# One set of scattering products for both small groups of the second layer's last part

## The chip, the cores and the metric

The kernel runs on one core of a Trainium2 chip. The metric is the device time of one execution in microseconds (us). TensorE (PE in the rows, PEld for its weight loads) multiplies matrices into PSUM; VectorE (DVE) and ScalarE (ACT) move and compute between PSUM and SBUF; SyncE (SP) issues the transfers between HBM and SBUF.

## The reference, cut to what matters

An attention over 4 samples of 576 tokens with 8 heads is followed by two mixture-of-experts layers of width 512 with 8 experts each. The second layer is the one that the change touches:

```python
logits = xc @ w_gate                    # xc: the tokens with x @ w_skip > 0
e_idx = np.argmax(logits, axis=1)
...
for e in range(E):
    mask = e_idx == e
    h = np.maximum(xc[mask] @ w1[e], 0.0)
    y[mask] = gate_w[mask, None] * (h @ w2[e])
out[do_compute] = xc + y
```

Each token goes to one expert; the result is weighted with the gate and added to the token.

## The kernel before

The samples are worked on one at a time, with the tokens along the free dimension: a sample's activations are X[b], four feature chunks of 128 partitions by 576 tokens. For each layer and sample the experts that got many tokens are *large groups* (class Group): all 576 tokens are multiplied with such an expert's weights, in 16 *slots* of 24 products of 288 columns, and the result is masked with the gate. Each factor is split into a high and a low part, which makes three products per block (hh, hl, wh, wl, xh, xl). The products of a slot go to one of two PSUM pairs, which ACT (hh) and then DVE (hl) evacuate.

Experts with at most 32 tokens are *small groups* (class Small). "S" is that of the first layer for sample 2 and has one expert (n = 1), "T" that of the second layer for sample 2 and has two (n = 2). Their words, in order: p (one-hot tile), g0 to g4 and gx (gather the tokens into xs), t (an expert's two layers in five steps), v (places: tiles that say where each token belongs), a (place: transposes them to pT), u (put: scatter the results). In t step 4 the expert's result is copied to two tiles, y2[0] (high part) and y2[1] (the rest). An expert's second layer leaves four blocks of 32 rows in PSUM: the two halves of the contraction for feature chunks 0 and 1, then those for chunks 2 and 3. So y2[.][:, c] holds results in rows 0 to 63 for c = 0, 1 and in rows 64 to 127 for c = 2, 3; the other half of the rows is zero from the start. put(t, i) takes chunks 2i and 2i + 1: for each and each half of the tokens it makes two products (high part, rest) of 288 columns against pT[t] into a bank of PSUM, and DVE adds that bank to X. The banks of put, of the transposes and of the router come from one pool of three (bank).

What stands where is a table written by hand, COURSE: one stage per large group, 16 lines per stage, one for each slot. Per slot: the 24 products, the split of the weights two slots later, the words ahead of the bar, the evacuation of the slot, the words behind the bar. Each engine works in that order. L4 to L7 load weights of the large group; O0 to O2 store chunks of samples; C3.x are the steps of the router for sample 3 (C3.1 logits, C3.2 transposes ptl, C3.3 one-hot oh, C3.4 counting products pp); G.1 and G.2 bring the gate into place (pgm, gT, mg); i.rw and kw prepare the router of sample 3. This document counts slots from 0, in the last stage (large group of layer 2, sample 1). The lines of that stage which speak of T are, before:

```python
    L4 G.3 | T.t03 O0.2
    | T.a0 i.rw
    L5 | T.t04 C3.1
    T.v1 | T.t10 T.u00
    L6 | T.u01 C3.2 G.1
    C3.3 | T.t11 C3.4 O0.3
    L7 C3.5 G.2 | T.t12 T.a1
    | T.t13
...
    | T.u10
    | T.u11 O1.0
```

These are slots 0 to 7, and 10 and 11 (T.t14 is in slot 9). T.v0 stands in slot 15 of the stage before. The tokens' weights of the small experts come in eight tiles each (tw, three buffers); a tile's load is issued when the product that read an earlier one is done.

Of the kernel before, what the change touches and what calls it, by code (L numbers as in the profile page):

```python
# [9 lines left out]
F32 = mybir.dt.float32  # L10
# [3 lines left out]
ALU = mybir.AluOpType  # L14
# [3 lines left out]
P = 128  # L18
NJ = 5
LAST = 64  # L20
HT = 288
TINY = 32
# [71 lines left out]
    N2 g.qn S.v0 | S.t03  # L94
    X2 | S.a0 g.qt
    N3 | S.t04
    X3 | S.u00 S.u01
    """),
    ((1, 0), """
    L4 G.3 | g.rw  # L100
# [17 lines left out]
    L4 G.3 | T.t03 O0.2  # L118
    | T.a0 i.rw
    L5 | T.t04 C3.1  # L120
    T.v1 | T.t10 T.u00
    L6 | T.u01 C3.2 G.1
    C3.3 | T.t11 C3.4 O0.3
    L7 C3.5 G.2 | T.t12 T.a1
    | T.t13
    Z B |
    | T.t14
    | T.u10
    | T.u11 O1.0
    | O2.0  # L130
    | O1.1 O2.1
    | O2.2
# [6 lines left out]
def kernel(  # L139
# [17 lines left out]
    nc = tc.nc  # L157
    B, H, S, D = q.shape
# [23 lines left out]
    def bank(name):  # L182
        return pa.tile([P, 512], F32, name=name, tag="a")

    def long_bank(name):

        return pb.tile([P, 512], F32, name=name, tag="b")
# [17 lines left out]
    def tokens(a):  # L205
        return slice(a * HT, (a + 1) * HT)
# [7 lines left out]
    iota = c32[:, C_IOTA:C_IOTA + TINY]  # L214
# [9 lines left out]
    for i, g in enumerate((w_gate, w_gate2)):  # L224
        t = cp.tile([P, NC, 32], F32, name=f"wg{i}")
        nc.gpsimd.memset(t, 0.0)
        with nc.allow_non_contiguous_dma(reason="gate weights are small"):
            nc.scalar.dma_start(out=t[:, :, 0:E], in_=g.rearrange("(c p) e -> p c e", p=P))
            if i == 1:
                nc.scalar.dma_start(  # L230
                    out=t[:, :, E:E + 1], in_=w_skip.rearrange("(c p o) -> p c o", p=P, o=1)
# [22 lines left out]
    for i in range(2):  # L254
        t = cp.tile([P, 2, P], F32, name=f"kvd{i}")
# [691 lines left out]
    with tc.tile_pool(name="fp", bufs=1) as fp:  # L947
# [3 lines left out]
        a, b = [Half(0, hh, X[0], fp, 1) for hh in range(2)]  # L951
# [158 lines left out]
    hp = ctx.enter_context(tc.tile_pool(name="hp", bufs=1, reuse_waits="tile"))  # L1110
    hp = ctx.enter_context(tc.tile_pool(name="hp", bufs=1, reuse_waits="tile"))
# [7 lines left out]
    class Small:  # L1119
# [69 lines left out]
        def expert(self, t, step):  # L1189
            if step == 0:  # L1190
                self.ph = long_bank("ph")
            elif step == 3:
                self.ph = long_bank("py")
            if step != 2:
                for i in {0: (0, 1), 1: (2, 3), 3: (4, 5), 4: (6, 7)}[step]:
                    w = self.tw.pop(8 * t + i)
                    for g in range(4):
                        if i < 4:
                            lhsT, rhs = self.xs[:, i, 32 * t:32 * t + 32], w[:, 256 * g:256 * g + 256]
                        else:  # L1200
                            lhsT = self.hT[:, g % 2, 32 * (i - 4):32 * (i - 4) + 32]
                            rhs = w.rearrange("p (u d) -> p u d", u=2)[:, g % 2, 256 * (g // 2):256 * (g // 2) + 256]
                        nc.tensor.matmul(  # L1203
                            out=self.ph[32 * g:32 * g + 32, :256], lhsT=lhsT, rhs=rhs, start=(i % 4 == 0), stop=(i % 4 == 3)
                        )
                    self.load(8 * t + i + 3)
            if step == 1:
                self.h1 = hp.tile([P, 256], F32, name="h1", tag="h1")
                nc.scalar.activation(self.h1, self.ph[:, :256], AF.Relu)
            elif step == 2:  # L1210
                pt = bank("pth")
                for u in range(2):
                    nc.tensor.transpose(pt[:, u * P:(u + 1) * P], self.h1[:, u * P:(u + 1) * P], ident)
                self.hT = hp.tile([P, 2, P], F32, name="hT", tag="h1")
                nc.vector.tensor_copy(out=self.hT, in_=pt[:, :2 * P].rearrange("p (u s) -> p u s", u=2))
            elif step == 4:
                for i in range(2):
                    sl, cs = slice(64 * i, 64 * i + 64), slice(2 * i, 2 * i + 2)
                    src = self.ph[sl, :256].rearrange("p (c d) -> p c d", c=2)
                    nc.scalar.copy(y2[0][sl, cs], src)  # L1220
                    nc.vector.tensor_sub(y2[1][sl, cs], src, y2[0][sl, cs].bitcast(F32))

        def places(self, t):
            cs = hp.tile([P, TINY], F32, name="cs2", tag="cs2")
            nc.vector.tensor_scalar(out=cs, in0=iota, scalar1=self.r["tlo"][:, t:t + 1], scalar2=None, op0=ALU.add)
            self.p4 = hp.tile([P, NJ, 4, TINY], F32, name="p4", tag="ot", bufs=3)
            bb = [P, NJ, TINY]
            for g in range(4):
                nc.vector.tensor_tensor(
                    out=self.p4[:, :, g],  # L1230
                    in0=self.r["z"].unsqueeze(2).to_broadcast(bb),
                    in1=cs.unsqueeze(1).to_broadcast(bb),
                    op=ALU.is_equal,
                )

# [8 lines left out]
            nc.tensor.transpose(pt[:, 0:LAST], p4f[:LAST, 4], ident[:LAST, :LAST])  # L1244
            nc.scalar.copy(pT[:, 4 * P:S], pt[:, 0:LAST])

        def put(self, t, i):
            for c in (2 * i, 2 * i + 1):
                for a in range(2):
                    pt = bank("pts")  # L1250
                    for n, u in enumerate(y2):
                        nc.tensor.matmul(  # L1252
                            out=pt[:, :HT], lhsT=u[:, c], rhs=self.pT[t][:, tokens(a)], start=(n == 0), stop=(n == 1)
                        )
                    x = self.x[:, c, tokens(a)]
                    nc.vector.tensor_add(x, x, pt[:, :HT])
# [83 lines left out]
    for kk, (_, plan) in enumerate(COURSE):  # L1340
        lines = plan.strip().split("\n")
        assert len(lines) == NS
        for i, line in enumerate(lines):
            before, _, after = line.partition("|")
            groups[kk].products(i)
            n = NS * kk + i + 2
# [131 lines left out]
```

## Time and profile before

| | us |
|---|---|
| runs timed | 424.27, 425.94, 426.3 (median 425.94) |
| the profiled execution | 423.36 |
| its span, first to last instruction | 421.5 |
| PE busy in the span | 396.1 (94%) |
| DVE busy | 251.8 (60%) |
| ACT busy | 182.5 (43%) |
| scattering products (L1252), 48 in all | 9.0 busy |

Sixteen of the 48 scattering products belong to S, 32 to T. Busy time of PE counts overlapping matmuls, whose ends are modelled; where PE is the bound, what a piece of work costs is read from the starts in the timeline: from its own start to that of the next kind of work on PE. Idle time stands in square brackets behind a row, with the engine whose end came last before it; that engine is inferred.

### The profile page before, as it was taken

To read this page: it belongs to the slowest core of one execution; us is meant where nothing else is said; L and a number is where in the kernel's file an instruction comes from. 1 tells how busy PE (TensorE), PEld (TensorE's weight loads), DVE (VectorE), ACT (ScalarE), POOL (GpSimd) and SP (SyncE) were. 2 spreads that over 40 slices of the span, in tenths; PEclk is the share of its full clock that TensorE was granted. 3 is DMA by queue.
4 is the path that set the end of the run, shared out by engine and by line. 5 is a ranking of instruction groups with operands and counts; after the bars stand their busy time and mean duration, and the time that the engine had idled before them with its cause. 6 is when DMAs were issued, how large, how long until landed. Compare 5 with 4: busy or idle time off the path is not lost.

```text
span 421.5 us, 8456 instructions
## 1 busy us (share of the span) xinstructions
PE 396.1 (94%) x3241; PEld 351.3 (83%) x3241; DVE 251.8 (60%) x640; ACT 182.5 (43%) x547; POOL 12.3 (3%) x46
## 2 busy tenths in 40 slices
PE   8989879999999999998999999998999999899893
PEld 4656779898999889798999888798998987799882
DVE  3875788463686755378446746367676736554431
ACT  1556666634257771423347523332375333231111
POOL 2400000000000000000000100000000000000000
PEclk9999999999999999999999999999999999999997
DMA  8819935200960300392544861117315555363134
GB/s 199 221 51 255 235 93 163 58 2 2 310 159 25 106 2 2 111 291 68 163 166 151 241 180 51 50 52 231 98 51 180 178 178 174 92 212 145 30 90 110
DMA packets 72536, 54.48 MB, mean 129 GB/s; under 512 B 18455, under 2 KB 67115, under 8 KB 72491
## 3 DMA queue, kind: packets, MB, share of 16 engines
q1 hardware_dynamic: 70536, 53.60, 44.1%
q10 hardware_dynamic: 1954, 0.31, 0.5%
q8 instruction: 26, 0.43, 0.4%
q14 instruction: 20, 0.16, 0.1%
HBM read 49.16 MB, written 4.73 MB: 128 GB/s over the span
## 4 chain that ended last, share of the span: by engine, by line
PE 70%; DVE 6%; ACT 3%; issue 2%; DVEq 0%; ACTq 0%
PE pair L860 29%; PE pair L839 21%; PE pxs L1147 2%; PE pk L437 2%; PE pl L593 2%; PE pto L1281 2%; PE ph L1203 1%; PE py L1203 1%; PE pts L1252 1%; PE px L495 1%; ACT hh L873 1%; PE ptq L463 1%; DVE wl L782 1%; PE ptx L1162 1%; DVE hl L874 1%
## 5 line engine op out<-in xcount | busy, mean ns | idle before, releaser
L860 PE MATMUL pair<-hh,wh 128*128 128x288 f32 x320 | 98.2, 307 | 0.0
L860 PE MATMUL pair<-hh,wl 128*128 128x288 f32 x320 | 94.4, 295 | 0.0
L860 PE MATMUL pair<-hl,wh 128*128 128x288 f32 x320 | 94.4, 295 | 0.0
L839 PE MATMUL pair<-xh,wh 128*128 128x288 f32 x304 | 92.9, 305 | 0.0
L839 PE MATMUL pair<-xl,wh 128*128 128x288 f32 x304 | 89.6, 295 | 0.0
L839 PE MATMUL pair<-xh,wl 128*128 128x288 f32 x304 | 89.4, 294 | 0.0
L782 DVE TENSOR_TENSOR wl<-ws,wh 128x512 fp32r<-128x512 f32 x80 | 54.9, 686 | 36.4 <-ACT wh L781 34.8
L873 ACT ACTIVATE hh<-pair 128x576 fp32r<-128x576 f32 x40 | 25.9, 647 | 88.6 <-PE pair L839 86.8
L860 PEld LDWEIGHTS pair<-hh,wh 128*128 128x128 f32 x320 | 60.4, 189 | 3.8 <-issue 2.6
L860 PEld LDWEIGHTS pair<-hl,wh 128*128 128x128 f32 x320 | 60.6, 189 | 0.1
L860 PEld LDWEIGHTS pair<-hh,wl 128*128 128x128 f32 x320 | 60.4, 189 | 0.0
L839 PEld LDWEIGHTS pair<-xh,wh 128*128 128x128 f32 x304 | 57.0, 188 | 2.3 <-issue 0.9
L874 DVE SCALAR_TENSOR_TENSOR hl<-pair,hh 128x576 fp32r<-128x576 f32 x40 | 30.2, 756 | 46.4 <-ACT hh L873 46.4
L839 PEld LDWEIGHTS pair<-xl,wh 128*128 128x128 f32 x304 | 57.1, 188 | 0.1
L839 PEld LDWEIGHTS pair<-xh,wl 128*128 128x128 f32 x304 | 57.1, 188 | 0.0
L781 ACT CAST wh<-ws 128x512 fp32r<-128x512 f32 x80 | 49.3, 620 | 2.6 <-DMA ws<-in_moe_w_dram 1.7
L334 ACT ACTIVATE eq<-qt,mx 128x64 f32<-128x64 f32 x140 | 46.7, 338 | 0.3 <-DVE mx L323 0.3
L334 ACT ACTIVATION_READ_ACCUMULATOR eq<-qt,mx 128x1 f32 x140 | 26.6, 190 | 0.0
L532 PE MATMUL pair<-warm 128*128 128x384 f16 x94 | 19.7, 359 | 1.6 <-DVE warm L949 1.6
L782 DVE TENSOR_TENSOR xl<-x,xh 128x576 fp32r<-128x576 f32 x20 | 14.9, 752 | 6.0 <-ACT xh L781 6.0
L1282 ACT COPY ot<-pto 128x256 f32<-128x256 f32 (+1 forms) x24 | 7.0, 316 | 26.0 <-PE pto L1281 26.0
L532 PEld LDWEIGHTS <-warm 128*128 128x128 f16 x94 | 9.6, 107 | 8.8 <-issue 3.2
(210 smaller groups left out, 499.9 us busy)
## 6 DMA issues: line engine op xcount, KB each, us to landing
ws<-in_moe_w_dram SPq DMA_DIRECT2D x39, 512.0 KB, 5.4
tw<-in_moe_w_dram SPq DMA_DIRECT2D x24, 512.0 KB, 4.1
kt<-in_k_dram SPq DMA_DIRECT2D x8, 512.0 KB, 7.7
qt<-in_q_dram SPq DMA_DIRECT2D x8, 512.0 KB, 6.8
out_dram<-ot SPq DMA_DIRECT2D x12, 256.0 KB, 2.7
vt<-in_v_dram SPq DMA_DIRECT2D x16, 128.0 KB, 4.5
vt<-in_v_dram SPq DMA_DIRECT2D x3, 512.0 KB
mg<-gate SPq DMA_DIRECT2D x4, 288.0 KB, 6.1
```

Source lines behind the costliest of these rows:

```text
L334: nc.scalar.activation(self.eqv[:, h, j], self.qt[:, h, j], AF.Exp, bias=self.mx[:, i:i + 1], accum_out=self.qz[:, i:i + 1])
L437: nc.tensor.matmul(out=pk[64 * g:64 * g + 64, c * D1 + o:c * D1 + o + n], lhsT=self.kt[:rows(j), 2 * c + g, j], rhs=ones32[:rows(j), 0:1] ...
L532: nc.tensor.matmul(out=pw[:, 0, :3 * P], lhsT=warm16[:, 0:P], rhs=warm16, start=True, stop=True)
L593: nc.tensor.matmul(out=pl[32 * c:32 * c + 32, :HT], lhsT=self.weights[:, c], rhs=self.chunk(c, tokens(a)), start=True, stop=True,)
L781: nc.scalar.copy(hi, src)
L782: nc.vector.tensor_tensor(out=lo, in0=src, in1=hi.bitcast(F32), op=ALU.subtract)
L839: nc.tensor.matmul(out=self.pt[:, a, :HT], lhsT=u[:, c], rhs=w[:, c, tokens(a)], start=(c == 0 and n == 0), stop=(c == NC - 1 and n == 2),)
L860: nc.tensor.matmul(out=self.pt[:, a, :HT], lhsT=p_[:, f], rhs=w[:, tokens(a)], start=(v == 0 and f == 0 and n == 0), stop=(v == 1 and f == ...
L873: nc.scalar.activation(halves(hh), src, AF.Relu)
L874: nc.vector.scalar_tensor_tensor(out=halves(hl), in0=src, scalar=0.0, in1=halves(hh).bitcast(F32), op0=ALU.max, op1=ALU.subtract,)
L1147: nc.tensor.matmul(out=self.px[:, c * self.w:(c + 1) * self.w], lhsT=self.xt[:rows(j), c * P:(c + 1) * P], rhs=self.pj[:rows(j), j], start ...
L1203: nc.tensor.matmul(out=self.ph[32 * g:32 * g + 32, :256], lhsT=lhsT, rhs=rhs, start=(i % 4 == 0), stop=(i % 4 == 3))
```

## The change

The results of T's two experts share the tiles y2. For the second expert (t = 1) the second layer writes its four blocks of rows in the order 3, 4, 1, 2, so that its results lie in the rows that the first expert's leave at zero: rows 64 to 127 for chunks 0 and 1, rows 0 to 63 for chunks 2 and 3. The places follow: v0 and v1 no longer make one tile per expert but one per pair of chunks (v0 for chunks 0 and 1 with the first expert in rows 0 to 63, v1 for chunks 2 and 3 with the second there), each from the index tiles of both experts. put(i) then multiplies y2 once with pT[i] for both experts. In the table, put of the first expert leaves slots 3 and 4, and u0 and u1 stand where u10 and u11 stood. For S nothing is different.

```diff
-    X3 | S.u00 S.u01
+    X3 | S.u0 S.u1
...
-    T.v1 | T.t10 T.u00
-    L6 | T.u01 C3.2 G.1
+    T.v1 | T.t10
+    L6 | C3.2 G.1
...
-    | T.u10
-    | T.u11 O1.0
+    | T.u0
+    | T.u1 O1.0
...
                     for g in range(4):
+
+                        o = 32 * (g ^ 2 if t and i >= 4 else g)
...
-                            out=self.ph[32 * g:32 * g + 32, :256], lhsT=lhsT, rhs=rhs, start=(i % 4 == 0), stop=(i % 4 == 3)
+                            out=self.ph[o:o + 32, :256], lhsT=lhsT, rhs=rhs, start=(i % 4 == 0), stop=(i % 4 == 3)
...
-                    sl, cs = slice(64 * i, 64 * i + 64), slice(2 * i, 2 * i + 2)
+                    o = 64 * (i ^ t)
+                    sl, cs = slice(o, o + 64), slice(2 * i, 2 * i + 2)
...
-            cs = hp.tile([P, TINY], F32, name="cs2", tag="cs2")
-            nc.vector.tensor_scalar(out=cs, in0=iota, scalar1=self.r["tlo"][:, t:t + 1], scalar2=None, op0=ALU.add)
+            cs = hp.tile([P, 2, TINY], F32, name="cs2", tag="cs2")
+            for u in range(self.n):
+                nc.vector.tensor_scalar(
+                    out=cs[:, u], in0=iota, scalar1=self.r["tlo"][:, u:u + 1], scalar2=None, op0=ALU.add
+                )
...
-                    in1=cs.unsqueeze(1).to_broadcast(bb),
+                    in1=cs[:, (g // 2) ^ t if self.n == 2 else 0].unsqueeze(1).to_broadcast(bb),
...
-        def put(self, t, i):
+        def put(self, i):
+            pT = self.pT[i if self.n == 2 else 0]
...
-                            out=pt[:, :HT], lhsT=u[:, c], rhs=self.pT[t][:, tokens(a)], start=(n == 0), stop=(n == 1)
+                            out=pt[:, :HT], lhsT=u[:, c], rhs=pT[:, tokens(a)], start=(n == 0), stop=(n == 1)
```

On PE in slot 3, before: ph is the first layer of the second expert, pts a bank of the scattering products (y0 and y1 are y2's two tiles), pair the large group's PSUM pair.

```order
L1203 MATMUL ph_4252<-tw_4090,xs_3790 32x256 x4
L1203 MATMUL ph_4252<-tw_4190,xs_3790 32x256 x4
L1252 MATMUL pts_4265<-pT_4136,y0_637 128x288
L1252 MATMUL pts_4265<-pT_4136,y1_638 128x288
L1252 MATMUL pts_4269<-pT_4136,y0_637 128x288
L1252 MATMUL pts_4269<-pT_4136,y1_638 128x288
L1252 MATMUL pts_4273<-pT_4136,y0_637 128x288
L1252 MATMUL pts_4273<-pT_4136,y1_638 128x288
L1252 MATMUL pts_4277<-pT_4136,y0_637 128x288
L1252 MATMUL pts_4277<-pT_4136,y1_638 128x288
L839 MATMUL pair1_84<-xh_124,wh0_202 128x288
```

The same place after:

```order
L1205 MATMUL ph_4254<-tw_4091,xs_3790 32x256 x4
L1205 MATMUL ph_4254<-tw_4191,xs_3790 32x256 x4
L839 MATMUL pair1_84<-xh_124,wh0_202 128x288
L839 MATMUL pair1_84<-xl_125,wh0_202 128x288
L839 MATMUL pair1_84<-xh_124,wl0_206 128x288
```

The eight scattering products between the expert's first layer and the large group's products of slot 4 are gone.

On PE at the end of slot 4, before: behind the slot's products come the second set of scattering products, the router's transposes (ptl), the gate transpose (pgm), and the products of slot 5.

```order
L1252 MATMUL pts_4312<-pT_4136,y0_637 128x288
L1252 MATMUL pts_4312<-pT_4136,y1_638 128x288
L1252 MATMUL pts_4316<-pT_4136,y0_637 128x288
L1252 MATMUL pts_4316<-pT_4136,y1_638 128x288
L1252 MATMUL pts_4320<-pT_4136,y0_637 128x288
L1252 MATMUL pts_4320<-pT_4136,y1_638 128x288
L1252 MATMUL pts_4324<-pT_4136,y0_637 128x288
L1252 MATMUL pts_4324<-pT_4136,y1_638 128x288
L605 MATMUL ptl_4328<-c32_85,lp_4202 128x128 x4
L607 MATMUL ptl4_4333<-c32_85,lp_4202 64x128
L915 MATMUL pgm_4337<-c32_85,gm_4067 5x128
L839 MATMUL pair0_83<-xh_124,wh1_203 128x288
```

The same place after:

```order
L839 MATMUL pair1_84<-xl_125,wh0_202 128x288
L839 MATMUL pair1_84<-xh_124,wl0_206 128x288
L605 MATMUL ptl_4298<-c32_85,lp_4203 128x128 x4
L607 MATMUL ptl4_4303<-c32_85,lp_4203 64x128
L915 MATMUL pgm_4307<-c32_85,gm_4068 5x128
L839 MATMUL pair0_83<-xh_124,wh1_203 128x288
L839 MATMUL pair0_83<-xl_125,wh1_203 128x288
```

The router's transposes stand directly behind the products of slot 4.

On DVE from slot 3 to the start of slot 5, before: cs and p are the place tiles, hl the evacuation, wl the split of weights, x the addition of a bank to X, L and gT the router's and the gate's results.

```order
L1225 TENSOR_SCALAR cs_4241<-c_85,tlo_183 128x32
L1229 TENSOR_TENSOR p_4243<-z_180,cs_4241 128x5x32 x4
L874 SCALAR_TENSOR_TENSOR hl<-pair_83,hh 128x576
L1256 TENSOR_TENSOR x_123<-x_123,pts 128x288 x4
L782 TENSOR_TENSOR wl_208<-ws_201,wh_204 128x512
L874 SCALAR_TENSOR_TENSOR hl<-pair_84,hh 128x576
L1256 TENSOR_TENSOR x_123<-x_123,pts 128x288 x4
L608 TENSOR_REDUCE L<-ptl 128x64
L614 TENSOR_REDUCE L<-ptl_4333 64x16
L917 COPY gT<-pgm 5x128
L782 TENSOR_TENSOR wl_209<-ws_201,wh_205 128x512
```

The same stretch after:

```order
L1229 TENSOR_SCALAR cs_4242<-c_85,tlo_183 128x32 x2
L1235 TENSOR_TENSOR p_4245<-z_180,cs_4242 128x5x32 x4
L874 SCALAR_TENSOR_TENSOR hl<-pair_83,hh 128x576
L782 TENSOR_TENSOR wl_208<-ws_201,wh_204 128x512
L874 SCALAR_TENSOR_TENSOR hl<-pair_84,hh 128x576
L608 TENSOR_REDUCE L<-ptl 128x64
L614 TENSOR_REDUCE L<-ptl_4303 64x16
L917 COPY gT<-pgm 5x128
L782 TENSOR_TENSOR wl_209<-ws_201,wh_205 128x512
```

The two blocks of four additions are gone, and the second index tile is added to the first.

## Rows read from the trace of the kernel before

**Rows 1.** The page's part 1 and the groups by line: busy, mean ns | idle before
```profile
PE 396.1 (94%) x3241; PEld 351.3 (83%) x3241; DVE 251.8 (60%) x640; ACT 182.5 (43%) x547; POOL 12.3 (3%) x46
L1252 PE MATMUL pts<-pT,y 128*128 128x288 f32 x48 | 9.0, 314 | 2.8 <-DVE x L1256 2.7
```

**Rows 2.** Timeline, end of slot 3: start us, us, engine, line, operation [idle before]
```profile
353.87 1.07 PE L1203 MATMUL ph<-tw,xs 128*32 128x256 f32 x16
...
354.65 0.76 DVE L874 SCALAR_TENSOR_TENSOR hl<-pair,hh 128x576 fp32r<-128x576 f32 x1 [0.59 <-ACT hh L873]
354.87 0.83 PEld L1252 LDWEIGHTS pts<-pT,y 128*128 128x128 f32 x6 [0.41 <-ACT hh L873]
354.87 1.62 PE L1252 MATMUL pts<-pT,y 128*128 128x288 f32 x8
...
355.95 0.30 PEld L1252 LDWEIGHTS pts<-pT,y 128*128 128x128 f32 x2 [0.25 <-DVE x L1256]
...
356.32 0.29 PE L839 MATMUL pair<-xh,wh 128*128 128x288 f32 x1
...
356.45 0.29 PE L839 MATMUL pair<-xl,wh 128*128 128x288 f32 x1
```

**Rows 3.** Timeline, end of slot 4
```profile
359.50 0.96 PE L1252 MATMUL pts<-pT,y 128*128 128x288 f32 x6
...
360.38 0.76 DVE L874 SCALAR_TENSOR_TENSOR hl<-pair,hh 128x576 fp32r<-128x576 f32 x1 [2.79 <-ACT hh L873]
361.05 1.54 DVE L1256 TENSOR_TENSOR x<-x,pts 128x288 f32<-128x288 f32 x4
...
361.55 0.53 PE L1252 MATMUL pts<-pT,y 128*128 128x288 f32 x2 [1.10 <-DVE x L1256]
...
361.92 0.66 PE L605 MATMUL ptl<-c,lp 128*128 128x128 f32 x4
...
362.64 0.08 PEld L915 LDWEIGHTS pgm<-c,gm 128*5 128x5 f32 x1 [0.23 <-DVE x L1256]
...
362.67 0.38 PE L839 MATMUL pair<-xh,wh 128*128 128x288 f32 x1
```

**Rows 4.** Timeline, end of slot 7, and the groups of tile tw (ns min/median/max)
```profile
375.93 1.07 PE L1203 MATMUL py<-tw,hT 128*32 128x256 f32 x16
...
376.92 0.19 PEld L860 LDWEIGHTS pair<-hh,wh 128*128 128x128 f32 x1 [0.41 <-ACT hh L873]
...
377.16 0.29 PE L860 MATMUL pair<-hl,wh 128*128 128x288 f32 x1
...
L1203 PE MATMUL py<-tw,hT x48: 379/379/403, 348.5 to 384.2; 128*32 128x256 f32 x48
```

**Rows 5.** Timeline, the router of sample 3 in slots 4 and 5
```profile
362.61 0.42 DVE L608 TENSOR_REDUCE L<-ptl 128x64 f32<-128x256 f32 x1
...
363.28 0.67 DVE L782 TENSOR_TENSOR wl<-ws,wh 128x512 fp32r<-128x512 f32 x1
...
364.79 0.20 DVE L632 TENSOR_TENSOR oh<-sc,fm 128x40 f16<-128x40 f32 x1
...
367.03 0.27 PE L644 MATMUL pp<-oh,c 128*128 128x32 f16 x4
```

**Rows 6.** Timeline and tile tw between 354 and 357: a weight tile for slot 5
```profile
354.56 0.33 SPq L1181 DMA_DIRECT2D tw<-in_moe_w_dram  x1
...
DMA to landing us min/median/max: 3.8/3.8/3.8
...
366.02 1.07 PE L1203 MATMUL ph<-tw,xs 128*32 128x256 f32 x16
```

**Rows 7.** Timeline of DVE, the place step of slot 3 and behind that of the stage before
```profile
352.76 0.23 DVE L1225 TENSOR_SCALAR cs<-c,tlo 128x32 f32<-128x32 f32 x1
...
336.26 0.69 DVE L782 TENSOR_TENSOR wl<-ws,wh 128x512 fp32r<-128x512 f32 x1 [0.69 <-ACT wh L781]
```

**Rows 8.** Timeline, the last two scattering products of slot 11
```profile
394.48 0.53 PE L1252 MATMUL pts<-pT,y 128*128 128x288 f32 x2 [1.22 <-DVE x L1256]
```

## The prediction

> **What bounds the kernel now.** I read the page first. TensorE (PE) is busy for 94% of the span [rows 1] and no other engine comes near. The time before is therefore set by the order of work on PE and by the few places where PE waits. The page's mean for one scattering product, 314 ns [rows 1], is not what such a product costs: matmuls are pipelined, and in the timeline a product of the same 288 columns starts 0.13 us after the one before it (356.32, then 356.45) [rows 2]. So I went to the timeline of the two slots from which products are removed, slots 3 and 4 of the last stage, and read when PE's next kind of work starts. That gives the price of the removed work with its waits.
>
> In slot 3, expert products of T end a block that starts at 353.87; the scattering products start at 354.87, the fourth pair of them waits for a PSUM bank, and the large group's products resume at 356.32 [rows 2]. In slot 4 six scattering products go out from 359.50, then PE stands still for 1.10 us: all three banks of the rotating pool are full, and the additions that empty them stand on VectorE (DVE) behind the hl evacuation (360.38, 0.76 us), so the first starts at 361.05. The last two products start at 361.55, and the router's transposes (ptl) at 361.92 [rows 3]. Both slots lie on PE, with no other engine ahead of it.
>
> **What the change removes.** 16 scattering products and 8 additions on DVE leave slots 3 and 4. Slots 10 and 11 keep 8 products each, on the same operands in size, with the same additions; their costs, a stop of 1.22 us in slot 11 included [rows 8], stay.
>
> Slot 3. What will stand behind the expert products is the large group's first product. The same succession is there in slot 7 of before: expert products at 375.93, and the second of the products behind them at 377.16, that is 1.23 us after [rows 4]. (The second is taken because the first after such a switch lasts longer.) In slot 3 that gives 353.87 + 1.23 = 355.10 where 356.45 stands now: 1.35 us gained. Of this 8 x 0.13 = 1.04 us is streaming and the rest the wait for a bank.
>
> The 0.41 us in front of the scattering products is put down to ACT [rows 2], which would make it a wait that goes with them. In slot 7 the large group's own products have the same 0.41 us behind expert products [rows 4]. I therefore keep it. The Trainium skill says the same in "TensorEngine Tiling (Array Packing)", section Tiling Modes, Key Properties: changing the tiling mode drains TensorE. By the label in slot 3 the gain would be 0.41 us larger, by that rule and the row of slot 7 it is not.
>
> Slot 4. The transposes for the router take the place of the first scattering product: 361.92 - 359.50 = 2.42 us gained. The gate transpose (pgm) after them waited 0.23 us for the last addition [rows 3]; its bank will then be one that was emptied long before, so 0.23 us more may go. I take 2.5, with 2.42 and 2.65 as ends.
>
> Sum on PE: 1.35 + 2.5 = 3.85 us, rounded 3.9. The 8 additions, in slot 4 a block of 1.54 us [rows 3], add nothing to it; what PE waited for them is in the sum. The lower bound is streaming alone, 16 x 0.13 = 2.1 us, if all the waits come back somewhere else; the upper one is 1.35 + 0.41 + 2.65 = 4.4 us.
>
> **What the change adds.** Each of T's two place steps makes two small index tiles on DVE instead of one: 0.23 us each [rows 7], 0.46 us in all. In slot 3 the next evacuation on DVE waited 0.59 us for ACT [rows 2], which hides it. The other one is at the end of the stage before, where DVE idles for 0.69 us ahead of its split at 336.26 [rows 7]. I cost both at nothing; uncovered they would cost at most 0.46 us. The second expert's second layer writes its four blocks of 32 rows in the order 3, 4, 1, 2 instead of 1, 2, 3, 4, and its results go to the other half of the rows of y. Count and size of these instructions stay. No row shows that order by itself; the order is the same cycle begun elsewhere, so I take zero, between nothing and the price of the third rival.
>
> **Who waits next.** From slot 5 on PE is 3.9 us early. Three things must be in time. The router's counting products (pp) wait for the one-hot tile oh, whose chain on DVE ran from 363.28 to 364.99, while pp came at 367.03 [rows 5]. In the new order that chain follows the slot's evacuation, which follows PE: hl would end at 360.38 + 0.76 - 1.35 = 359.8, the two reductions and the gate copy of slot 4 take 0.7 us (362.61 to 363.28), the chain 1.7 us: oh ready at about 362.2. PE wants it at 367.03 - 3.9 = 363.1. It is in time, with 0.9 us left. The weights of the second expert for slot 5 were issued at 354.56 and landed in 3.8 us, at 358.4; they are wanted at 366.02 - 3.9 = 362.1 [rows 6]. In time by 3.7 us. All later loads are issued by what PE or DVE finish from slot 5 on and move with them.
>
> At the end, slots 10 to 15 and the stores keep their order, so the whole gain reaches the last store.
>
> **The forecast.** The profiled execution took 423.36 us, its span 421.5. Less 3.9 it is 419.5. The three timed runs have a median of 425.94, above the profiled one; the mean of all four is 425.0. The gain from the median gives 422.0, from the mean 421.1. I put 421.6 between them: faster by about 0.9%.
>
> **Rivals.**
> 1. *Half the gain is given back in slot 5.* If the oh chain kept its present time (ready at 364.99) instead of moving with PE, pp would wait until then: 365.0 - 363.1 = 1.9 us returned, 2.0 us of gain left, 423.5 on the forecast's basis. For it: the margin is only 0.9 us, and the chain also has DVE's weight split before it. Against: nothing in the rows ties that chain to a fixed time; it now starts right behind the additions that go. It comes out much the same if only the streaming, 2.1 us, is gained.
> 2. *The loads become the bound.* If the tile issued at 354.56 landed later than 7.5 us after its issue, PE would stop in slot 5 for the excess, up to all 3.9 us: 421.6 to 425.5. Against: it landed in 3.8 us [rows 6], and nothing about its neighbours in the queue changes.
> 3. *Slower: the second expert's blocks no longer overlap.* 16 expert products of 0.379 us each are issued in a block of 1.07 us, since neighbours go to different blocks of 32 columns [rows 2, 4]. If the changed order lost that, they would take 16 x 0.379 = 6.1 us, 5.0 us more in each of slots 7 and 9: 10.0 - 3.9 = 6.1 us slower, 431.6. It decides once more than 1.95 us per block is lost. Against: neighbours still go to different blocks, and a block returns after four products as before.
> 4. *The saving is larger.* If the 0.41 us of slot 3 and the 0.23 us of slot 4 both went, 4.4 us: 421.1. That lies in the forecast's own range.
>
> That the change does not do what it says has no room: the order on PE shows the 16 products gone from the two slots and nothing put in their place.
>
> **How the numbers follow.** Forecast (3.4 to 4.4 us gained) 0.80, with the fourth rival in it; first rival 0.08; second 0.07; third 0.05. The range: the gain's own bounds, 3.4 to 4.4, around the two bases 425.94 and 425.0, give 420.6 to 422.5; the runs shown spread by 2 us (424.27 to 426.3), so about 1.3 us more on the low side gives 419.3; above, the first rival's 423.5 and a little of the spread give 424.2. Left out are the second rival's worse half and the third: under 2 in 10. A measurement of this kernel can tell about 0.5%, 2.1 us, from no change. The forecast and part of the first rival's spread lie beyond that: faster 0.80; the rest of the first and the second, same 0.15; the third, slower 0.05.
>
> **What would show it.** In the changed kernel's timeline the product after the expert products of slot 3 should start 1.0 us after their start, with the 0.41 us still in front of it; the router's transposes should follow slot 4's products at once, with no stop on PE until the large group's next product, about 0.6 us later; pp in slot 5 should have no wait on DVE; from slot 5 to the last store every piece should keep its distance from the one before it. In slots 7 and 9 the blocks of expert products should still last about 1.07 us. The forecast is wrong if PE stands still at ptl, pp or the expert products of slot 5, or if a later stop (slots 11 to 15) grows by what was gained.

## The result and the profile after

The changed kernel took 419.88 us (median of four runs, 419.13 to 420.29) against 425.11 for the kernel before (four runs, 423.6 to 426.3): ratio 0.9897, 95% interval 0.9873 to 0.9921, so about 1% faster. In a second comparison the ratio was 0.9883 (0.9858 to 0.9909). The profiled execution took 419.54 us; its span is 3.9 us shorter than that of before. Runs of one kernel spread with their mean granted clock (of eleven runs of the kernel before in the second comparison, seven at 0.990 to 0.994 took 423.7 to 424.4 us and four at 0.985 to 0.986 took 425.8 to 426.5), so the 5.2 us between the two medians is not the gain of the change alone; that is read from the traces.

The head of the page of the changed kernel, which answers to the table before:

```profile
span 417.6 us, 8418 instructions
...
PE 393.2 (94%) x3225; PEld 349.2 (84%) x3225; DVE 249.1 (60%) x634; ACT 182.4 (44%) x547; POOL 12.2 (3%) x46
```

PE is still the bound at 94%. It is busy 2.9 us less (by modelled ends) while the span is 3.9 us shorter, so idle time went too. Where it went stands in the timeline of the changed kernel, PE in slots 3 to 6 (start us, us, engine, line, operation), which answers to [rows 2, 3, 5]:

```profile
353.78 1.07 PE L1205 MATMUL ph<-tw,xs 128*32 128x256 f32 x16
354.78 0.40 PE L839 MATMUL pair<-xh,wh 128*128 128x288 f32 x1
...
358.07 0.60 PE L605 MATMUL ptl<-c,lp 128*128 128x128 f32 x4
...
358.64 0.38 PE L839 MATMUL pair<-xh,wh 128*128 128x288 f32 x1
...
361.99 1.07 PE L1205 MATMUL ph<-tw,xs 128*32 128x256 f32 x16
363.00 0.27 PE L644 MATMUL pp<-oh,c 128*128 128x32 f16 x4
...
367.57 0.38 PE L1215 MATMUL pth<-c,h 128*128 128x128 f32 x2
```

No row has idle time in brackets. Slot 4's first products come 1.00 us behind the expert products, its transposes (ptl) follow its last product at once, and slot 5 starts 0.57 us after them. From the expert products of slot 3 to the first product of slot 5 it is 358.64 - 353.78 = 4.86 us. Before it was 8.80 us (353.87 [rows 2] to 362.67). The gain in these two slots is 3.94 us.

I use two distances from here on, since spans of single executions of one kernel differ by up to 1 us through something that lies before slot 3 (the last section shows it). **D1** is this one. **D2** runs from the same expert products to the last group of five output transposes (pto) that starts without a wait, by PE before and then after:

```profile
411.88 0.71 PE L1281 MATMUL pto<-c,x 128*128 128x128 f32 x5
```

```profile
407.86 0.71 PE L1288 MATMUL pto<-c,x 128*128 128x128 f32 x5
```

Before it is 353.87 to 411.88, 58.01 us; after 353.78 to 407.86, 54.08 us. The gain at the end is 3.93 us: nothing was given back on the way.

DVE of the changed kernel in the same stretch: the place step, the evacuation behind it, and the end of the chain to oh.

```profile
352.68 0.38 DVE L1229 TENSOR_SCALAR cs<-c,tlo 128x32 f32<-128x32 f32 x2
...
354.57 0.76 DVE L874 SCALAR_TENSOR_TENSOR hl<-pair,hh 128x576 fp32r<-128x576 f32 x1 [0.44 <-ACT hh L873]
...
361.80 0.20 DVE L632 TENSOR_TENSOR oh<-sc,fm 128x40 f16<-128x40 f32 x1
```

The second index tile makes cs last 0.38 us where one lasted 0.23 [rows 7]; hl waits 0.44 us where it waited 0.59 [rows 2]. The addition came out of idle time, so it cost nothing. oh is done at 362.00, and PE asks for it at 363.00: a margin of 1.0 us.

The stop in slot 11 is where it was [rows 8], by PE and then DVE of the changed kernel:

```profile
388.26 0.95 PE L1259 MATMUL pts<-pT,y 128*128 128x288 f32 x6
390.43 0.53 PE L1259 MATMUL pts<-pT,y 128*128 128x288 f32 x2 [1.21 <-DVE x L1263]
390.80 1.20 PE L1288 MATMUL pto<-c,x 128*128 128x128 f32 x5
```

```profile
388.46 0.76 DVE L896 TENSOR_TENSOR yt<-pair,mg 128x576 f32<-128x576 f32 x1 [2.11 <-PE pair L860]
389.26 0.76 DVE L897 TENSOR_TENSOR x<-x,yt 128x576 f32<-128x576 f32 x1
389.93 1.54 DVE L1263 TENSOR_TENSOR x<-x,pts 128x288 f32<-128x288 f32 x4
```

Six products fill the three banks; the additions that empty them stand behind 1.5 us of evacuation. This is the pattern that the change took out of slot 4, and one copy of it is left.

### The profile page after: what moved, and what is told of

Its sections match the earlier page's. It is cut to its first block, busy times and chain, and to the rows that moved or that the text cites. A ratio compares the mean times of both kernels' runs of the same rounds, so it can differ in the third digit from the quotient of the medians.

```text
span 417.6 us, 8418 instructions
## 1 busy us (share of the span) xinstructions
PE 393.2 (94%) x3225; PEld 349.2 (84%) x3225; DVE 249.1 (60%) x634; ACT 182.4 (44%) x547; POOL 12.2 (3%) x46
## 4 chain that ended last, share of the span: by engine, by line
PE 70%; DVE 6%; ACT 3%; issue 2%; DVEq 0%; ACTq 0%
PE pair L860 30%; PE pair L839 21%; PE pxs L1147 2%; PE pk L437 2%; PE pl L593 2%; PE pto L1288 2%; PE ph L1205 1%; PE py L1205 1%; PE px L495 1%; PE ptq L463 1%; ACT hh L873 1%; PE pts L1259 1%; DVE wl L782 1%; PE ptx L1162 1%; DVE hl L874 1%
```

## The experiments

**Theory A**, the prediction's: what a set of scattering products costs depends on its place, streaming plus the wait for a bank there: 1.35 us in slot 3, 2.5 in slot 4. **Rival B**: the 16 products cost the same wherever they stand, 3.9 / 16 = 0.24 us each. They are told apart by taking each set out alone, by putting the products back without their additions, and by moving them to where DVE is free.

### One set taken out

From the kernel before; the first expert's results for two feature chunks are then never added.

```diff
-    T.v1 | T.t10 T.u00
+    T.v1 | T.t10
```

> The kernel before without the first put of the first expert (slot 3: 8 products, 4 additions; the first expert's results for chunks 0 and 1 are left out of the output). Measured in the trace from the start of the expert products of slot 3 to the first large-group product of slot 5: 8.80 us before, 4.86 us after. Theory A (what goes is what stood on TensorE: streaming and the waits of this place): 1.3 us less, 7.5 us, span 420.2. Theory B (each removed product is worth the same wherever it stands, 3.9 / 16 = 0.24 us): 1.95 us less, 6.85 us, span 419.5.

D1 was 7.46 us, 1.34 less than before, and D2 1.34 less. Ratio 0.9977 (0.996 to 0.9994). The end of slot 4, PE of this kernel, still has its stop:

```profile
359.06 0.95 PE L1252 MATMUL pts<-pT,y 128*128 128x288 f32 x6
361.12 0.53 PE L1252 MATMUL pts<-pT,y 128*128 128x288 f32 x2 [1.10 <-DVE x L1256]
361.48 0.66 PE L605 MATMUL ptl<-c,lp 128*128 128x128 f32 x4
```

The other set, with the first expert's results for the other two chunks left out:

```diff
-    L6 | T.u01 C3.2 G.1
+    L6 | C3.2 G.1
```

> The kernel before without the second put of the first expert (slot 4: 8 products, 4 additions; the first expert's results for chunks 2 and 3 are left out). Theory A: 2.6 us less (8 x 0.13 = 1.05 us streaming, 1.55 us waits for banks behind VectorE's evacuation): 6.2 us between the two marks, span 418.9. Theory B: 1.95 us less, 6.85 us, span 419.5.

D1 was 6.20 us, 2.60 less; D2 2.55 less. Ratio 0.9941 (0.9924 to 0.9957). PE at the end of its slot 3:

```profile
354.67 1.07 PE L1203 MATMUL ph<-tw,xs 128*32 128x256 f32 x16
...
357.11 0.30 PE L839 MATMUL pair<-xh,wh 128*128 128x288 f32 x1
```

They resume at 357.11, 2.44 us behind the start of the expert products, as before (353.87 to 356.32 [rows 2]). Equal numbers of equal products are worth 1.34 us in one slot and 2.55 in the other. B asked for the same from both; A holds. The two add up to 3.89 of the 3.93 us.

### The products without their additions

In the changed kernel the 16 products are put back in slots 3 and 4 (against the first place tile), and what they write is not added to anything:

```diff
-    T.v1 | T.t10
-    L6 | C3.2 G.1
+    T.v1 | T.t10 T.d0
+    L6 | T.d1 C3.2 G.1
...
+        def dry(self, i):
+            for c in (2 * i, 2 * i + 1):
+                for a in range(2):
+                    pt = bank("pts")
+                    for n, u in enumerate(y2):
+                        nc.tensor.matmul(out=pt[:, :HT], lhsT=u[:, c], rhs=self.pT[0][:, tokens(a)], ...)
```

> The changed kernel with the 16 scattering products put back in slots 3 and 4, into banks that nothing reads, without the 8 additions (the output is complete). It gives the price of the products alone. Theory A: streaming only, 16 x 0.13 = 2.1 us more than after: 7.0 us between the marks, span 419.7. Theory B in its form 'the products cost 0.24 us each': 3.9 us more, 8.8 us, span 421.5. A third reading, that the additions on VectorE were all of the price: 0 more, 4.9 us.

D1 was 6.95 us and D2 2.12 us more than in the changed kernel; ratio to before 0.9966 (0.9948 to 0.9984). PE of this kernel:

```profile
355.43 1.31 PE L1270 MATMUL pts<-pT,y 128*128 128x288 f32 x8
...
359.76 1.21 PE L1270 MATMUL pts<-pT,y 128*128 128x288 f32 x8
360.81 0.60 PE L605 MATMUL ptl<-c,lp 128*128 128x128 f32 x4
```

There is no wait, and eight products take 1.05 us (359.76 to 360.81), 0.13 each. Without waits the 16 cost 2.1 us. The other 1.8 us of the gain were waits for DVE's additions.

### The products where DVE is free

The kernel before, with nothing left out: the eight products of each set are issued a bank at a time. Two banks stay in slot 3, three go to slot 7 and three to slot 8; each "w" is one bank of put, two products and an addition.

```diff
-    T.v1 | T.t10 T.u00
-    L6 | T.u01 C3.2 G.1
+    T.v1 | T.t10 T.w000 T.w001
+    L6 | C3.2 G.1
...
-    | T.t13
-    Z B |
+    | T.t13 T.w010 T.w011 T.w020
+    Z B | T.w021 T.w030 T.w031
```

> The kernel before with the first expert's eight banks of scattering products spread, two behind slot 3, three behind slot 7, three behind slot 8, none in slot 4 (all work is done). No bank should be waited for then. Theory A: the waits go, 1.8 us, and the streaming of 2.1 us stays: 5.4 us between the marks, span 419.7. Theory B: nothing is removed, so span 421.5.

D1 5.41 us, and D2 1.77 us less than before; ratio 0.9964 (0.9945 to 0.9983). PE:

```profile
355.52 0.80 PE L1255 MATMUL pts<-pT,y 128*128 128x288 f32 x4
...
359.35 0.60 PE L605 MATMUL ptl<-c,lp 128*128 128x128 f32 x4
```

With all the work still done, moving it gains 1.77 us, the waits' share again from the other side. What is left to the changed kernel, 3.93 - 1.77 = 2.16 us, is 16 products of 0.135 us. So a little under half of the change's gain could be had by order alone.

### The same thought for the stop that is left

In the changed kernel the second set, u1, is put ahead of the bar in slot 11, that is ahead of the slot's evacuation, so that its additions stand first on DVE. The changed kernel ran beside it.

```diff
-    | T.u1 O1.0
+    T.u1 | O1.0
```

> The changed kernel with u1 of slot 11 ahead of the bar: TensorE's order is the same, on VectorE the four additions stand ahead of the slot's evacuation (multiplication with the gate and addition, 2 x 0.76 us). In after, from the first product of slot 11 to the first of slot 12: 6.8 us, with a stop of 1.2 us for a bank. Theory A: the stop shrinks to about 0.25 us as in slot 10, 5.8 us, span 416.6. Theory B (products and additions have a price of their own, their order none): span 417.6. Against A: the copy of the stored chunk on VectorE comes behind the evacuation, 1.5 us later than now, and could stop the transposes of slot 12.

> The changed kernel again, on the same chip as the last. Ratio to before 0.990, span 417.6.

The changed kernel repeated its distances to the digit (D1 4.86, D2 54.08; 419.79 us, six runs from 419.3 to 420.46). This one has D2 52.88, 1.20 less where 1.0 was expected, and took 418.73 us (six runs from 418.12 to 419.18): ratio to before 0.9862 (0.9837 to 0.9887). Every run of it is below every run of the changed kernel beside it, so it beats both kernels. PE and DVE at the end of its slot 11:

```profile
388.42 1.50 PE L1259 MATMUL pts<-pT,y 128*128 128x288 f32 x8
389.75 1.20 PE L1288 MATMUL pto<-c,x 128*128 128x128 f32 x5
```

```profile
388.88 1.55 DVE L1263 TENSOR_TENSOR x<-x,pts 128x288 f32<-128x288 f32 x4 [2.38 <-PE pts L1259]
390.34 0.75 DVE L896 TENSOR_TENSOR yt<-pair,mg 128x576 f32<-128x576 f32 x1
```

The stop of 1.21 us is gone, and the evacuation starts at 390.34 instead of 388.46 with nobody waiting for it: slot 13, which needs that PSUM pair again, starts without a wait. The output transposes (pto) have no wait either, so the objection in the expectation did not come true. The wait of [rows 8] was made by the order on DVE.

### How near the next wait is

The margin of the chain to oh, 1.0 us, was only read. In the changed kernel DVE was given four operations of 0.76 us on a tile that they leave as it is, ahead of the five operations that end in oh; 3.12 us of DVE in all.

```diff
-    C3.3 | T.t11 C3.4 O0.3
+    T.z C3.3 | T.t11 C3.4 O0.3
...
+        def idle(self):
+            for _ in range(4):
+                x = self.x[:, 0]
+                nc.vector.tensor_max(x, x, x)
```

> The changed kernel with four operations of 0.76 us each (a chunk's maximum with itself, which changes nothing) on VectorE in slot 5, ahead of the router's one-hot chain: 3.0 us. In after the one-hot tile is ready at 362.0 and the counting products start at 363.0. If that chain is what is late next (1.0 us margin), the counting products wait 2.0 us and the span is 419.6. If it has more room than read, or TensorE makes up for it later, less: 417.6 at the lowest.

pp did wait 2.03 us, as the margin says. But D2 grew by 4.93 us, not 2.0: the expectation failed. PE in slots 5 and 6 of this kernel, and below it the windows of the stop, of the small products behind it, and of slot 6's products (us, busy time of PE, PEld, DVE, ACT and POOL with counts, granted TensorE clock, DMA share, GB/s):

```profile
362.19 1.07 PE L1205 MATMUL ph<-tw,xs 128*32 128x256 f32 x16
365.29 0.29 PE L644 MATMUL pp<-oh,c 128*128 128x32 f16 x4 [2.03 <-DVE oh L632]
...
367.73 0.44 PE L839 MATMUL pair<-xl,wh 128*128 128x288 f32 x1
367.97 0.44 PE L839 MATMUL pair<-xh,wl 128*128 128x288 f32 x1
...
372.69 0.38 PE L1215 MATMUL pth<-c,h 128*128 128x128 f32 x2
```

```profile
362.10:365.20 3.10, 1.16 (x18) 0.42 (x16) 2.89 (x9) 1.03 (x2) 0.00 (x0) 0.99 0.40 66
365.20:367.30 2.10, 1.97 (x22) 1.51 (x23) 1.01 (x5) 0.37 (x1) 0.00 (x0) 0.50 1.02 392
367.30:371.80 4.50, 4.50 (x19) 4.50 (x20) 2.34 (x12) 0.78 (x2) 0.00 (x0) 0.50 0.50 135
```

Behind the stop the granted clock is 0.50, the lower of its two levels (1.2 instead of 2.4 GHz), and products of 288 columns start 0.24 us apart instead of 0.13, for 4.5 us. From ph to pth in slot 6 it takes 10.50 us, against 5.58 in the changed kernel (361.99 to 367.57). New theory: a stop at this place costs itself and then the clock. Three more executions varied the number of operations: two, three, and four again.

> The changed kernel, with two operations of 0.76 us put on VectorE ahead of the last step of the gate (oh) that pp of slot 5 waits for; the run before had four. oh comes 1.53 us later; the margin read from the trace is 1.0 us, so pp should wait some 0.5 us. From the start of ph to the start of pth of slots 5 to 6 the changed kernel takes 5.58 us. If a stop of 0.5 us costs only itself: 6.1. If the margin was misread: 5.6 or 7.1.

> The same with three operations: oh comes 2.3 us later, pp should wait some 1.3 us. If the stop costs only itself and the granted clock stays at its upper level, as in the stops of 1.10 and 1.22 us of the kernel before: from ph to pth 6.9 us. If TensorE's clock falls to its lower level behind it, as behind the stop of 2.0 us in the run with four operations: up to 9.5 us, with large-group products 0.24 us apart instead of 0.13.

> The run with four operations once more. If the fall of the granted clock behind the stop of 2.0 us belongs to the stop: from ph to pth 10.5 us again. If it was an accident of that one execution: 5.58 + 2.0 = 7.6 us.

| operations | pp waits | ph to pth | above the changed kernel's 5.58 | D2 above 54.08 |
|---|---|---|---|---|
| 2 | 0.46 | 6.52 | 0.94 | 0.94 |
| 3 | 1.25 | 8.84 | 3.26 | 3.25 |
| 4 | 2.03 | 10.50 | 4.92 | 4.93 |
| 4 again | 2.04 | 9.36 | 3.78 | 3.77 |

The rows of the wait, PE in the kernels with two and three operations:

```profile
363.90 0.27 PE L644 MATMUL pp<-oh,c 128*128 128x32 f16 x4 [0.46 <-DVE oh L632]
...
365.57 0.30 PE L1293 MATMUL pto<-c,x 128*64 128x128 f32 x1 [0.24 <-ACT ot L1294]
```

```profile
365.63 0.27 PE L644 MATMUL pp<-oh,c 128*128 128x32 f16 x4 [1.25 <-DVE oh L632]
```

The waits, 0.46, 1.25 and 2.04, step by about the 0.78 us of one operation, and they put the margin at 1.0 us, as read. With two operations the total is 0.94 where 0.5 was expected: a second wait follows, 0.24 us of the last output transpose for a bank, and slot 6's first product comes 1.73 us behind pp instead of 1.32. Its clock holds. With three, the wait of 1.25 us is followed by the lower level, and the expectation's upper case (up to 9.5) is nearer than its lower (6.9). Windows of that kernel (stop, small products, slot 6's first products) and then of the repeat with four:

```profile
363.30:365.60 2.30, 1.08 (x17) 0.42 (x16) 2.13 (x8) 1.03 (x2) 0.00 (x0) 1.00 0.21 22
365.60:367.30 1.70, 1.43 (x22) 1.12 (x22) 1.11 (x4) 0.37 (x1) 0.00 (x0) 1.00 0.87 334
367.30:370.90 3.60, 3.60 (x17) 3.60 (x18) 2.17 (x12) 0.78 (x2) 0.00 (x0) 0.55 0.63 206
```

```profile
366.30:368.20 1.90, 1.81 (x22) 1.34 (x23) 1.00 (x4) 0.37 (x1) 0.00 (x0) 0.76 1.00 388
368.20:370.50 2.30, 2.30 (x10) 2.30 (x11) 1.41 (x5) 0.78 (x2) 0.00 (x0) 0.50 0.40 124
```

The fall came in all three executions whose stop here was 1.25 us or more, so it was no accident of one. Its cost varies: the repeat with four came out between its two expectations (10.5 and 7.6), and the two executions with four operations differ by 1.2 us with the same wait, through the length of the slow stretch alone. These were single executions, so the sizes are those of one execution each. That a stop of this length brings the fall every time does not follow; the last section has stops of 2.1 us without it.

## Why the prediction was right

**Slot 3, 1.35 us.** Taking that set out alone gave 1.34. **Slot 4, 2.5 us** between 2.42 and 2.65: alone it gave 2.60 over these slots and 2.55 at the end. The term was a little small: of the 0.23 us in front of the gate transpose most went, since from ptl to slot 5 it is 0.57 us now and was 0.75 (361.92 to 362.67 [rows 3]). The method held: a price read from start to start of PE's next kind of work, at that place, its waits included. The page's mean duration would have given 16 x 0.314 = 5.0 us, and the streaming alone 2.1.

**The 0.41 us behind expert products** was kept, against its label. It is still there, and in slot 5 the same 0.41 us has another label. PEld of the changed kernel, slots 3 and 5:

```profile
354.78 0.19 PEld L839 LDWEIGHTS pair<-xh,wh 128*128 128x128 f32 x1 [0.41 <-ACT hh L873]
...
362.99 0.17 PEld L644 LDWEIGHTS <-c 128*128 128x128 f16 x4 [0.41 <-issue]
```

Whatever follows a block of expert products (scattering products before, large-group products, pp) starts 1.00 to 1.01 us after the block's start; only the label of the gap changes. The Trainium skill, "TensorEngine Tiling (Array Packing)", section Tiling Modes, Key Properties, says that a change of the tiling mode drains TensorE. The trace agrees, at 0.41 us here; no run separated the drain from another cause that comes with these blocks.

**The additional index tiles, nothing.** In slot 3 the wait of hl shrank from 0.59 to 0.44 us, and PE was not touched. Nor does the other place step show on PE: from the start of pp in an early stage to the expert products of slot 3 it is 295.15 us before and 295.13 after (58.72 to 353.87 and 58.65 to 353.78).

**Who waits next.** oh was forecast for 362.2 and wanted at 363.1; it came at 362.0 and was wanted at 363.0. The experiment on the margin confirmed the 1.0 us. The first rival, half of the gain given back there, did not happen. The expert products of slot 5 have no wait, so the second rival, late loads, did not happen either. For the third, the blocks of the second expert's second layer in slots 7 and 9, PE of the changed kernel:

```profile
371.89 1.07 PE L1205 MATMUL py<-tw,hT 128*32 128x256 f32 x16
...
379.45 1.07 PE L1205 MATMUL py<-tw,hT 128*32 128x256 f32 x16
```

They last 1.07 us as before [rows 4]: the changed order of the four column blocks costs nothing. Of the fourth rival's two terms the 0.41 us stayed and most of the 0.23 us went.

**The sum** of 3.9 us was 3.93 at the end, and the profiled execution came out at 419.54 where 419.5 was worked out. That the last figure fits so well is in part luck: both profiled executions kept the upper clock behind an early stop (last section), and a second traced execution of the changed kernel, which did not, has a span of 418.5 us instead of 417.6 with the same D1 and D2. What was off is the last step, from the profiled execution to a median. I put the forecast at 421.6, between two bases, 425.94 and 425.0, and the measured median is 1.7 us lower: both bases contain runs of 425.94 and 426.3 us, and none of the ten runs of the changed kernel in the two comparisons lies so far above its lowest one. At equal clock, 0.994, spans of before in the second comparison were 421.9 and 422.0 us, those of the changed kernel 417.5, 417.5 and 417.8: a difference of 4.1 to 4.5, near the 3.9 of the traces. What lowers the mean clock to 0.985 and 0.986 in some runs of the kernel before is open, for none of those runs was traced; a second fall of the clock of the kind in the last section would give about that much (0.987 in the repeat with four operations, which had two). Taking the stop in slot 4 out is not a sufficient cure, since the kernel with the products alone, which does not stop there, also had two runs of ten some 2 us above most of the others.

## What to carry to other kernels

Price a piece of work on the bounding engine from start to start, in its place: the same eight products were worth 1.3 us in one slot and 2.5 in the next, and the difference was what stood on another engine ahead of the additions that free their banks. Before work is taken out, look whether its waits go by order alone: issue it where the engine that frees a small pool of buffers has time (1.8 of 3.9 us here), or put the operations that free the pool ahead of a long evacuation that nobody waits for (1.2 us in slot 11). And compare two kernels by distances between marks in the traces when the gain is no larger than the spread of their runs.

## What the runs showed of the hardware

A stop of TensorE can cost more than itself. Where it stood still for 1.25 and 2.0 us between a block of expert products and the router's small products, the granted clock fell behind it to 0.50 (1.2 GHz), and large-group products started 0.24 us apart until it rose again. With two operations, where the clock held, D2 grew by 0.42 us more than pp came later (0.94 - 0.52), which goes with the second wait at the output transposes. With three it grew by 1.94 us more (3.25 - 1.31), with four by 2.84 and 1.67 (4.93 - 2.09 and 3.77 - 2.10). If the 0.42 us are in each of these, which the rows of the executions with four do not show, the lower clock cost 1.3 to 2.4 us, an estimate.

The length of the stop does not decide alone. In each of the twelve traced executions, whatever the kernel, pp also stops PE in an early stage, for 2.12 to 2.14 us and between the same pieces of work. The changed kernel was traced twice; PE at that stop and the window behind it (columns as above), first from the execution with a span of 417.6 us and then from the one with 418.5:

```profile
58.65 0.27 PE L644 MATMUL pp<-oh,c 128*128 128x32 f16 x4 [2.13 <-DVE oh L632]
60.00:62.00 2.00, 2.00 (x17) 2.00 (x16) 1.95 (x8) 1.34 (x9) 0.00 (x0) 1.00 0.46 136
```

```profile
58.14 0.27 PE L644 MATMUL pp<-oh,c 128*128 128x32 f16 x4 [2.12 <-DVE oh L632]
60.00:62.00 2.00, 2.00 (x10) 2.00 (x10) 1.90 (x10) 0.83 (x6) 0.00 (x0) 0.50 0.21 59
```

Behind the same stop the clock stayed at 1.00 in one and was 0.50 in the other. It fell in six of the twelve executions. In those six it is 296.6 to 296.7 us from this pp to the expert products of slot 3, in the other six 295.1: the fall cost 1.5 us each time. In the six with the fall pp started between 57.88 and 58.40 us of the span, in the others between 58.65 and 59.29. So the outcome goes with when the stop comes, while the work around it is the same; nothing was changed to test this.

Behind shorter stops the clock stayed at 1.00 in every traced execution: 0.46 us in slot 5, 1.09 to 1.14 us at pp in two later stages (all twelve executions), 1.10 us in slot 4 (two) and 1.21 or 1.22 us in slot 11 (eleven). Here are the windows of the kernel before around the stops in slots 4 and 11 [rows 3, 8]:

```profile
359.50:362.70 3.20, 2.10 (x17) 1.57 (x15) 2.30 (x6) 1.16 (x2) 0.00 (x0) 1.00 0.48 139
392.00:396.00 4.00, 2.68 (x18) 1.98 (x17) 3.30 (x7) 0.37 (x1) 0.00 (x0) 1.00 0.00 0
```

Both lie within scattering products of 288 columns, with transposes behind them. The single fall behind 1.25 us, beside eleven stops of 1.21 or 1.22 us without one, may thus be due to what PE does around the stop or to when it comes; these runs do not say which. The Trainium skill, "TensorE: Matmul & The Clock Gate", section "HAM oscillation — how this bites in real kernels", tells of a kernel whose waits between matmuls throttle TensorE again; the fall here, to 0.50 behind stops of 1.25 to 2.14 us, is of that kind. Margins of a microsecond on the bounding engine are thus worth keeping: in the one execution in which oh came 2.3 us later, 3.25 us of the 3.93 were given back.
